# A gated linear attention with a GEGLU block: phase sums in the attention's PSUM banks, and another order of the table phases

## The chip, the core and the metric

The kernel runs on one core of one Trainium2 chip. The time is that of the device for one execution, in microseconds (us); before the change its median over three executions is 323.64 us (323.56 to 323.77).

The core has engines that each take their own instructions in order and wait for each other through semaphores: TensorE (PE; its weight loads are listed as PEld) multiplies matrices into PSUM, VectorE (DVE) does elementwise arithmetic, ScalarE (ACT) evaluates functions from a table that has to be loaded first, GpSimd (POOL) and SyncE (SP) mostly start transfers here.

## The reference

Attention first: a recurrence over 768 steps with a complex decay per channel, for 4 batches and 8 heads of 48 channels.

```python
mag = sqrt(a_re**2 + a_im**2)
scale = minimum(mag, 0.999) / (mag + 1e-6)
ar, ai = a_re * scale, a_im * scale
for t in range(S):                              # S = 768
    S_re, S_im = ar[t]*S_re - ai[t]*S_im + outer(k[t], v[t]), ar[t]*S_im + ai[t]*S_re
    y[t] = q[t] @ S_re
```

Then, on x = y laid out as 3072 tokens of 384 features (hidden size 1536):

```python
ffn = (gelu(x @ w_gate) * (x @ w_val)) @ w_out
out = x + sigmoid(x @ w_res) * ffn
```

## The kernel before

The recurrence is done in chunks of 128 steps. The decay of a chunk is a product of complex numbers, so its logarithm is a running sum: of ln|a| for the size, of the angle for the phase. Running sums along the 128 steps are matmuls with triangular matrices (`csl` for the logarithms, `cst` for the phases). The size becomes `E` and `Ei` (exponentials of plus and minus the sum), the phase is reduced to one turn (`r`, `fg`) and becomes cosine and sine (`CS`). Queries and keys are multiplied by both (`qE`, `kE`, then `Q`, `K`), and what is left is ordinary linear attention: transposes (`tp`, copied as `qk`), scores (`at`, masked as `atm`), the output `y`, the carried state (`dk`, `G`, `Gb`). After that `x` is transposed to `xT` for the gates.

A group g is two chunks of 128 steps, and there are 12 groups, 3 to a batch (`NS = 3`). They are handled in 7 units: one group, five pairs, one group. ScalarE needs three tables: ln/exp, trigonometric, gelu. The program alternates `phase_x(u)`, which has the ln/exp and the trigonometric table, and `phase_y(u)`, which has gelu. In `phase_x(u)` there stand the decay work of units u+1 and u+2, the second half of the attention of unit u and the output projection (`op`) of unit u-1; in `phase_y(u)` the gates `gp` and `vp` of unit u and the first half of the attention of unit u+1.

All eight PSUM banks are given out:

```python
psM = tile_pool(name="psM", bufs=4, space=PSUM)   # tag "mm": csl, cst, ms, tpx, gp, vp, rp, op
psT = tile_pool(name="psT", bufs=1, space=PSUM)   # tp
psA = tile_pool(name="psA", bufs=1, space=PSUM)   # at
psY = tile_pool(name="psY", bufs=1, space=PSUM)   # y
psD = tile_pool(name="psD", bufs=1, space=PSUM)   # dk
```

The steps for one group's decay; `s0` to `s3` belong to the ln/exp table:

```python
def s0(): act(out=lm, in_=lm, func=AF.Ln)                       # ar <- ar
def s1():
    act(out=s, in_=lm, func=AF.Exp, scale=-1.0)                 # s <- ar
    nc.vector.tensor_tensor(out=th, in0=s, in1=th, op=OP.mult)  # ai <- s,ai   (L189)
def s2(): act(out=s, in_=th, func=AF.Square)                    # s <- ai
def s3():
    act(out=s, in_=s, func=AF.Ln, bias=1.0)
    nc.vector.scalar_tensor_tensor(out=lm, in0=s, scalar=0.5, in1=lm, ...)    # L197
    nc.vector.tensor_scalar(out=lm, in0=lm, scalar1=LNMAX, ..., op0=OP.min)   # L198

def p1_arctan(g): act(out=th, in_=th, func=AF.Arctan)           # ai <- ai, trigonometric table

def cs_l(g, c):
    cs = psM.tile([128, DM], FP, tag="mm", ...)
    nc.tensor.matmul(out=cs, lhsT=lmat[c], rhs=lm[:, sl], start=True, stop=True)
    def ex():
        act(out=E[:, sl], in_=cs, func=AF.Exp)
        act(out=Ei[:, sl], in_=cs, func=AF.Exp, scale=-1.0)
    return ex

def cs_t(g, c):
    if c == 0:
        T["fg", g] = pE.tile([128, C * H, 2, D], FP, tag="fg", name="fg")
    cs = psM.tile([128, DM], FP, tag="mm", ..., name="cst")
    nc.tensor.matmul(out=cs, lhsT=tmat[c], rhs=th[:, sl], start=True, stop=(s == 0))   # L236
    if s > 0:                                                    # carry of the group before
        nc.tensor.matmul(out=cs, lhsT=ones2pi, rhs=T["P", g], start=False, stop=True)  # L238
    nc.vector.tensor_scalar(out=r, in0=cs, scalar1=MAGIC, scalar2=MAGIC, op0=OP.add, op1=OP.subtract)
    nc.vector.tensor_tensor(out=fg[:, hs, 1, :], in0=cs, in1=r, op=OP.subtract)
    if c == C - 1:
        ...   # absolute value of fg into fg[:, :, 0, :]   (L246)

def p2_sin(g):   # two activations Sin: CS[:, :, 0] and CS[:, :, 1] from fg
```

The attention of a chunk; each of these steps is issued with high priority, so that a scheduler moves it ahead of other work as soon as its inputs and buffers allow:

```python
def a():   # grp(hg), four heads
    tp = psT.tile([128, 1024], BF, tag="tp")
    ...    # 8 transposes of Q and K, copied to qk: one half by ScalarE, one by VectorE
    at = psA.tile([128, 4, 128], FP, tag="at", name="at")
    ...    # 4 matmuls
    nc.vector.tensor_tensor(out=atm, in0=at, in1=mask4, op=OP.mult)      # L359
...
def yy():
    y = psY.tile([128, DM], FP, tag="y", ..., name="y")
    ...    # 8 or 16 matmuls
    nc.scalar.copy(out=x, in_=y)
return [hi(f) for f in (enter, grp(0), dk, grp(1), yy)]
```

The gates of unit u need the `xT` of all its chunks:

```python
def gv_step(u, ffi):   # 12 times a unit
    ...    # 3 matmuls gp, 3 matmuls vp, both in "mm" banks
    act(out=h2[:, ffi, :], in_=gp, func=AF.Gelu)
    nc.vector.scalar_tensor_tensor(out=h2[:, ffi, :], in0=h2[:, ffi, :], scalar=0.5, in1=vp, ...)
```

The order in which steps are issued comes from `weave`, which spreads each list of steps over a stretch of the phase (0 to 1) and sorts all by place:

```python
atn = [table("trig_and_small")] + [call(p1_arctan, g) for g in g2]
cst = [call(carry, g) for g in g1] + [call(cs_t, g, c) for g in g1 for c in range(C)]
sin = [call(p2_sin, g) for g in g1]
...
weave((0.0, 0.12, csls), (0.05, 0.5, zip_steps([p1(g) for g in g2])), (0.01, 0.01, dec1), (0.12, 0.45, exs),
      (0.46, 0.46, dec), (0.2, 0.65, cst), (0.7, 0.95, atn + sin), (0.95, 0.95, dec3), (0.0, 0.8, att), (0.1, 1.0, ops))
```

From unit 3 on, the factor that carries the state (`M`) is made from three rows that go through DRAM and back (`decay0` to `decay3`, in the lists `dec1`, `dec` and `dec3`).

Of the kernel before, what the change touches and what calls it, by code (L numbers as in the profile page):

```python
# [9 lines left out]
FP = mybir.dt.float32  # L10
# [6 lines left out]
def weave(*streams):  # L17

    order = []
    for si, (begin, end, steps) in enumerate(streams):  # L20
        n = len(steps)
        for i, step in enumerate(steps):
            order.append((begin + (end - begin) * (i + 0.5) / n, si, i, step))
    for _, _, _, step in sorted(order, key=lambda e: e[:3]):
        step()
# [3 lines left out]
def kernel(  # L29
# [14 lines left out]
    B, H, S, D = q.shape  # L44
    DD = 2 * D
    DM = H * D
# [3 lines left out]
    C = 2  # L50
    W = C * DM
# [44 lines left out]
    pS = ctx.enter_context(tc.tile_pool(name="pS", bufs=2))  # L96
    pE = ctx.enter_context(tc.tile_pool(name="pE", bufs=2))
# [10 lines left out]
    psM = ctx.enter_context(tc.tile_pool(name="psM", bufs=4, space=PSUM))  # L108
    psT = ctx.enter_context(tc.tile_pool(name="psT", bufs=1, space=PSUM))
    psA = ctx.enter_context(tc.tile_pool(name="psA", bufs=1, space=PSUM))  # L110
    psY = ctx.enter_context(tc.tile_pool(name="psY", bufs=1, space=PSUM))
# [117 lines left out]
    def cs_t(g, c):  # L229
        s = g % NS  # L230
        th = T["th", g]
        if c == 0:
            T["fg", g] = pE.tile([128, C * H, 2, D], FP, tag="fg", name="fg")
        sl = slice(c * DM, (c + 1) * DM)
        cs = psM.tile([128, DM], FP, tag="mm", padded_shape=[128, 512], name="cst")
        nc.tensor.matmul(out=cs, lhsT=tmat[c], rhs=th[:, sl], start=True, stop=(s == 0))  # L236
        if s > 0:
            nc.tensor.matmul(out=cs, lhsT=ones2pi, rhs=T["P", g], start=False, stop=True)  # L238
        cs3 = cs.rearrange("p (h d) -> p h d", h=H)
        fg = T["fg", g]  # L240
        hs = slice(c * H, (c + 1) * H)
        r = pS.tile([128, H, D], FP, tag="r", name="r")
        nc.vector.tensor_scalar(out=r, in0=cs3, scalar1=MAGIC, scalar2=MAGIC, op0=OP.add, op1=OP.subtract)
        nc.vector.tensor_tensor(out=fg[:, hs, 1, :], in0=cs3, in1=r, op=OP.subtract)
        if c == C - 1:
            nc.vector.tensor_scalar(out=fg[:, :, 0, :].bitcast(mybir.dt.int32), in0=fg[:, :, 1, :].bitcast(mybir.dt.int32),  # L246
                                    scalar1=0x7FFFFFFF, scalar2=None, op0=OP.bitwise_and)
# [37 lines left out]

    def sums(g):
        ms = psM.tile([128, H], FP, tag="mm", padded_shape=[128, 512], name="ms")
        two = pS.tile([128, W], FP, tag="s", name="two")

        def half(gg, c):  # L290
            sl = T["lm", gg][:, c * DM:(c + 1) * DM].rearrange("p (h u d) -> p h u d", u=1, d=D)
            return sl.to_broadcast([128, H, 2, D])
        nc.vector.tensor_tensor(out=two.rearrange("p (h u d) -> p h u d", u=2, d=D), in0=half(g - 1, 1),
                                in1=half(g, 0), op=OP.add)
        for h in range(H):
            nc.tensor.matmul(out=ms[0:DD, h:h + 1], lhsT=two[:, h * DD:(h + 1) * DD], rhs=ones1,
                             start=(h == 0), stop=(h == H - 1), skip_group_check=True)
        T["ms", g] = mp.tile([128, H], FP, tag="ms", name="msb")
        nc.vector.tensor_copy(out=T["ms", g][0:DD], in_=ms[0:DD])
# [175 lines left out]
    def table(nm):  # L475
        def f():
            tab(nc.scalar.preload_act_table_set(nm))  # L477
        return f

    def gs(u):  # L480
        return UNITS[u] if 0 <= u < NU else []
# [7 lines left out]
    def call(f, *a):  # L489
        return lambda: f(*a)  # L490

    def zip_steps(lists):
        return [st[i] for i in range(max(map(len, lists), default=0)) for st in lists if i < len(st)]
# [14 lines left out]
    def phase_x(u):  # L508

        pend = []  # L510
        g1, g2 = gs(u + 1), gs(u + 2)
        d1 = [g for g in g1 if g % NS > 0 and g > NEAR]
        ops = [call(op_step, u - 1, jj) for jj in range(len(gs(u - 1)) * C)]
        att = att_steps(u, 1)
        if not g1:
            weave((0.0, 0.8, att), (0.1, 1.0, ops))
            return

        def csl(g, c):
            pend.append(cs_l(g, c))  # L520

        def ex():
            pend.pop(0)()

        def p1(g):
            return p1_steps(g) + ([call(decay0, g)] if g % NS > 0 and g > NEAR else [])
        csls = [call(csl, g, c) for g in g1 for c in range(C)]
        exs = [ex for _ in g1 for _ in range(C)]
        dec = [call(decay2, g) for g in d1]
# [3 lines that stand above are left out]
        dec1 = [call(decay1, g) for g in d1]  # L533
        dec3 = [call(decay3, g) for g in d1]
        table("natural_log_exp_and_others")()
        if u < 0:
            for f in [st for g in g1 for st in p1(g)] + csls + exs:
                f()
            for f in atn[:1] + [call(p1_arctan, g) for g in g1] + cst + sin:
                f()  # L540
            return
        dec3 += [call(sums_exp, g) for g in g1 if g % NS > 0 and g <= NEAR]
        if u == 0:
            sm = [[call(sums, g) for g in gg if g % NS > 0] for gg in (g1, g2)]
            weave((0.0, 0.25, zip_steps([p1(g) for g in g1])), (0.26, 0.3, csls), (0.31, 0.32, sm[0]), (0.35, 0.45, exs),
                  (0.4, 0.64, zip_steps([p1(g) for g in g2])), (0.641, 0.642, dec3), (0.645, 0.65, atn[:1]),
                  (0.65, 0.66, [call(p1_arctan, g) for g in g1]), (0.67, 0.85, cst), (0.75, 0.8, atn[1:]),
                  (0.9, 0.95, sin), (0.96, 0.97, sm[1]), (0.0, 0.5, att))
            return
        if u == 1:  # L550
            for f in dec3:
                f()
            dec3 = []
        weave((0.0, 0.12, csls), (0.05, 0.5, zip_steps([p1(g) for g in g2])), (0.01, 0.01, dec1), (0.12, 0.45, exs),
              (0.46, 0.46, dec), (0.2, 0.65, cst), (0.7, 0.95, atn + sin), (0.95, 0.95, dec3), (0.0, 0.8, att), (0.1, 1.0, ops))

    def phase_y(u):

# [34 lines left out]
    for u in range(-1, NU + 1):  # L593
        phase_x(u)
        while u >= 0 and T["a"] < min(NG, gs(u + 1)[-1] + 6 if gs(u + 1) else NG):
            load_a(T["a"])
        phase_y(u)
        for g in gs(u + 3):
            load_q(g)
            after_landing(T["k", g], call(load_v, g))  # L600
# [30 lines left out]
```

## Time and profile before

| stretch (us from the start) | what it is | length |
|---|---|---|
| 0 to 24 | first group's loads and decay | 24.0 |
| 24 to 63.2 | ln/exp and trigonometric tables of u = 0 | 39.2 |
| 63.2 to 83.5 | gelu table of u = 0 | 20.3 |
| 83.5 to 101.4, to 127.8 | table phase of u = 1, its gelu table | 17.9, 26.4 |
| 127.8 to 147.0, to 173.0 | the same for u = 2 | 19.2, 26.0 |
| 173.0 to 192.6, to 219.0 | u = 3 | 19.6, 26.4 |
| 219.0 to 236.3, to 262.6 | u = 4 | 17.3, 26.3 |
| 262.6 to 274.7, to 297.9 | u = 5 | 12.1, 23.2 |
| 297.9 to 322.4 | last projections and unit 6 | 24.5 |

The profiled execution spans 322.4 us. The stretches are those between the loads of ScalarE's tables (line L477), of which there are 21 of 1.283 us each.

A line of a group of instructions names line, engine, operation and tiles, then how many there are, their busy time and the mean of one in ns, and then the idle time of the engine just before them with what ended most of it. A line of the list of waits names who waited, for whom, the sum in us, how many times, and sometimes the longest. A releaser is inferred, and idle time of an engine that nobody waits for costs nothing.

### The profile page before, as it was taken

The numbers are of one execution on the slowest core, as the hardware profiler recorded it, in microseconds if no ns is written. First come the engines' busy times: TensorE is split into PE (matmuls) and PEld (weight loads), VectorE is DVE, ScalarE is ACT, GpSimd is POOL, SyncE is SP. The second block draws the span as 40 slices with busy tenths as digits, with TensorE's granted clock in tenths as the row PEclk, the third lists the DMA queues.
The fourth block names the chain that finished last, engine by engine and source line by source line (L and its number), as shares of the span: only waits on it lengthen the run. The fifth ranks groups of instructions, "written<-read, shape, count | busy, mean of one in ns | idle before, by whom it ended". The sixth has DMA issues, their size and how long they took to land.

```text
span 322.4 us, 5853 instructions
## 1 busy us (share of the span) xinstructions
PE 272.1 (84%) x2200; PEld 170.5 (53%) x2200; DVE 234.8 (73%) x431; ACT 209.8 (65%) x353; POOL 80.5 (25%) x115
## 2 busy tenths in 40 slices
PE   0337927789887999789997999998999999899994
PEld 0116624677543666445664556554656655555682
DVE  2446769968499995599982999974899837864352
ACT  4549684646998557977568976569665683656150
POOL 1206522022040370259020572000630003200220
PEclk9995676959999999999999999999999999999998
DMA  8999999989999995396850595000360003600441
GB/s 159 218 183 181 182 169 165 185 174 180 187 179 186 223 160 33 76 197 113 122 36 2 107 121 95 2 0 3 75 122 3 2 0 76 122 2 0 107 91 50
DMA packets 137755, 34.55 MB, mean 107 GB/s; under 512 B 126848, under 2 KB 137728, under 8 KB 137728
## 3 DMA queue, kind: packets, MB, share of 16 engines
q1 hardware_dynamic: 103296, 23.60, 36.8%
q0 software_dynamic: 34432, 10.59, 31.2%
q8 instruction: 17, 0.28, 0.3%
q14 instruction: 10, 0.08, 0.1%
HBM read 31.31 MB, written 9.07 MB: 125 GB/s over the span
## 4 chain that ended last, share of the span: by engine, by line
PE 56%; SPq 12%; ACT 11%; DMA 9%; DVE 6%; issue 3%; POOL 1%; ACTq 0%; DVEq 0%; POOLq 0%
PE vp L443 14%; PE gp L439 13%; SPq L136 6%; SPq L144 6%; PE op L463 6%; DMA k<-in_k_dram 4%; PE rp L455 3%; PE tp L349 3%; PE tp L346 3%; PE at L356 3%; ACT L477 3%; DMA m<-dm 3%; ACT s L124 3%; PE cst L236 2%; PE y L394 2%
## 5 line engine op out<-in xcount | busy, mean ns | idle before, releaser
L124 ACT ACTIVATE h<-gp 128x512 bf16<-128x512 f32 (+1 forms) x84 | 44.5, 536 | 38.4 <-PE gp L439 37.9
L439 PE MATMUL gp<-xT,wg 128*128 128x512 bf16 (+1 forms) x252 | 65.4, 353 | 3.4 <-ACT h L124 2.0
L443 PE MATMUL vp<-xT,wv 128*128 128x512 bf16 (+1 forms) x252 | 66.6, 353 | 0.0
L446 DVE SCALAR_TENSOR_TENSOR h<-h,vp 128x512 bf16<-128x512 bf16 (+1 forms) x84 | 49.8, 603 | 16.4 <-PE vp L443 12.0
L463 PE MATMUL op<-wo,h 128*128 128x384 bf16 x288 | 50.2, 326 | 8.1 <-ACT Ei L124 5.9
L463 PEld LDWEIGHTS <-h 128*128 128x128 bf16 x288 | 27.8, 98 | 28.7 <-issue 11.3
L351 ACT COPY qk<-tp 96x512 bf16<-96x512 bf16 x48 | 27.9, 580 | 17.1 <-PE tp L349 7.9
L359 DVE TENSOR_TENSOR atm<-at,mask 128x512 bf16<-128x512 f32 x48 | 32.9, 686 | 8.2 <-PE at L356 7.8
L472 POOL DMA_DIRECT2D out_dram<-x x22 | 20.4, 947 | 54.4 <-DMA out_dram<-ot 43.1
L439 PEld LDWEIGHTS <-wg 128*128 128x128 bf16 x252 | 23.7, 99 | 17.9 <-issue 4.2
L443 PEld LDWEIGHTS <-wv 128*128 128x128 bf16 x252 | 23.8, 99 | 13.3
L189 DVE TENSOR_TENSOR ai<-s,ai 128x768 f32<-128x768 f32 x12 | 11.1, 955 | 23.6 <-ACT s L124 23.6
L477 ACT ACT_TABLE_LOAD x21 | 26.9, 1283 | 1.1 <-PEq L615 0.7
L346 PE MATMUL tp<-ident,Q 128*96 128x128 bf16 x192 | 20.1, 231 | 6.9 <-DVE Q L321 6.2
L346 PEld LDWEIGHTS <-Q 128*96 128x96 bf16 x192 | 17.4, 130 | 15.3 <-DVE Q L321 10.0
L124 ACT ACTIVATE CS<-fg,hpi 128x768 bf16<-128x768 f32 x12 | 11.2, 935 | 20.8 <-DVE fg L246 20.7
L150 POOL DMA_DIRECT2D v<-in_v_dram x24 | 21.9, 932 | 4.2 <-DMA v<-in_v_dram 1.3
L349 PE MATMUL tp<-ident,K 128*96 128x128 bf16 x192 | 22.3, 235 | 0.0
L236 PE MATMUL cst<-ai,lt0b 128*128 128x384 f32 x24 | 11.8, 577 | 11.7 <-ACT ai L124 11.0
L352 DVE COPY qk<-tp 96x512 bf16<-96x512 bf16 x48 | 19.8, 413 | 2.3 <-ACT qk L351 1.7
L212 PE MATMUL csl<-ar,lt0a 128*128 128x384 f32 x24 | 11.4, 562 | 10.8 <-DMA ar<-in_a_re_dram 10.8
L466 DVE SCALAR_TENSOR_TENSOR ot<-sg,op 128x384 f32<-128x384 f32 x24 | 13.1, 547 | 10.1 <-PE op L463 10.1
(85 smaller groups left out, 522.0 us busy)
## 6 DMA issues: line engine op xcount, KB each, us to landing
ar<-in_a_re_dram SPq DMA_DIRECT2D x24, 192.0 KB, 4.7
ai<-in_a_im_dram SPq DMA_DIRECT2D x24, 192.0 KB, 4.1
q<-in_q_dram SPq DMA_DIRECT2D x24, 192.0 KB, 3.8
k<-in_k_dram SPq DMA_DIRECT2D x24, 192.0 KB, 3.7
out_dram<-ot SPq DMA_DIRECT2D x24, 192.0 KB, 2.5
out_dram<-x POOLq DMA_DIRECT2D x22, 192.0 KB, 3.7
v<-in_v_dram POOLq DMA_DIRECT2D x24, 96.0 KB, 5.0
wg<-in_moe_w_gate_dram POOLq DMA_DIRECT2D x4, 288.0 KB, 11.4
```

Of the source, the lines that this page charges most:

```text
L124: tab(nc.scalar.activation(**kw))
L150: nc.gpsimd.dma_start(out=t[:, c], in_=rows(v, g, c))
L346: nc.tensor.transpose(out=tp[0:DD, j * 128:j * 128 + 128], in_=Q(x), identity=ident)
L349: nc.tensor.transpose(out=tp[0:DD, 512 + j * 128:640 + j * 128], in_=K(x), identity=ident)
L351: nc.scalar.copy(out=qk[0:DD, 0:512], in_=tp[0:DD, 0:512])
L359: nc.vector.tensor_tensor(out=atm, in0=at, in1=mask4, op=OP.mult)
L439: nc.tensor.matmul(out=gp, lhsT=wg[:, fi, ffi * 128:(ffi + 1) * 128], rhs=xT[:, fi, :], start=(fi == 0), stop=(fi == KD - 1))
L443: nc.tensor.matmul(out=vp, lhsT=wv[:, fi, ffi * 128:(ffi + 1) * 128], rhs=xT[:, fi, :], start=(fi == 0), stop=(fi == KD - 1))
L446: nc.vector.scalar_tensor_tensor(out=h2[:, ffi, :], in0=h2[:, ffi, :], scalar=0.5, in1=vp, op0=OP.mult, op1=OP.mult)
L463: nc.tensor.matmul(out=ps, lhsT=h2[:, ffi, jj * 128:(jj + 1) * 128], rhs=wo[:, ffi, :], start=(ffi == 0), stop=(ffi == KF - 1))
L472: nc.gpsimd.dma_start(out=out[t0:t0 + 128, :], in_=T["x", token(u, jj)], accum_op=OP.add)
L477: tab(nc.scalar.preload_act_table_set(nm))
```

## The change

The phase sums leave the four shared banks. A group's first half goes to the bank of `at`, its second half to that of `y`, so that it need not wait for `csl` to be read. The temporary `two` of the sums of the first units takes a buffer of `fg` in place of one of `s`. And the table phases are woven differently: attention is listed first, exponentials lead the ln/exp table, the phase sums come early, the decay of the unit after next follows, and in the trigonometric table the sines stand ahead of the arctangents.

```diff
@@ cs_t
-        cs = psM.tile([128, DM], FP, tag="mm", padded_shape=[128, 512], name="cst")
+        if c == 0:
+            cs = psA.tile([128, 4, 128], FP, tag="at", name="cst").rearrange("p j t -> p (j t)")[:, 0:DM]
+        else:
+            cs = psY.tile([128, DM], FP, tag="y", padded_shape=[128, 512], name="cst")
@@ sums
-        two = pS.tile([128, W], FP, tag="s", name="two")
+        two = pE.tile([128, C * H, 2, D], FP, tag="fg", name="two").rearrange("p x u d -> p (x u d)")[:, 0:W]
@@ phase_x, u == 0
-            weave((0.0, 0.25, zip_steps([p1(g) for g in g1])), (0.26, 0.3, csls), (0.31, 0.32, sm[0]), (0.35, 0.45, exs),
-                  (0.4, 0.64, zip_steps([p1(g) for g in g2])), (0.641, 0.642, dec3), (0.645, 0.65, atn[:1]),
+            p12 = zip_steps([p1(g) for g in g2])
+            weave((0.0, 0.25, zip_steps([p1(g) for g in g1])), (0.26, 0.3, csls), (0.31, 0.32, sm[0]), (0.32, 0.5, p12[:-2]),
+                  (0.5, 0.58, exs), (0.6, 0.64, p12[-2:]), (0.641, 0.642, dec3), (0.645, 0.65, atn[:1]),
                   (0.65, 0.66, [call(p1_arctan, g) for g in g1]), (0.67, 0.85, cst), (0.75, 0.8, atn[1:]),
                   (0.9, 0.95, sin), (0.96, 0.97, sm[1]), (0.0, 0.5, att))
@@ phase_x, u > 0
-        weave((0.0, 0.12, csls), (0.05, 0.5, zip_steps([p1(g) for g in g2])), (0.01, 0.01, dec1), (0.12, 0.45, exs),
-              (0.46, 0.46, dec), (0.2, 0.65, cst), (0.7, 0.95, atn + sin), (0.95, 0.95, dec3), (0.0, 0.8, att), (0.1, 1.0, ops))
+        weave((0.0, 0.8, att), (0.0, 0.04, csls), (0.01, 0.01, dec1), (0.04, 0.2, exs), (0.05, 0.3, cst), (0.21, 0.21, dec),
+              (0.2, 0.6, zip_steps([p1(g) for g in g2])), (0.62, 0.95, atn[:1] + sin + atn[1:]), (0.65, 0.65, dec3),
+              (0.25, 1.0, ops))
```

## The prediction

> **What bounds the kernel now.** I read the page first: the busy times and the 40 slices.
>
> ```profile
> PE 272.1 (84%) x2200; PEld 170.5 (53%) x2200; DVE 234.8 (73%) x431; ACT 209.8 (65%) x353; POOL 80.5 (25%) x115
> ...
> PE   0337927789887999789997999998999999899994
> DVE  2446769968499995599982999974899837864352
> ACT  4549684646998557977568976569665683656150
> PEclk9995676959999999999999999999999999999998
> ```
>
> TensorE is the fullest engine, but 50 us of the span are not its own. About 18 of them lie in the first 24 us, before there is anything to multiply. What the change can touch is the rest. So I cut the span at the 21 table loads of ScalarE (line L477): each unit u has a ln/exp table, a trig table (together the "table phase") and a gelu table. The windows view of two such phases, each with the ln/exp part cut in two and the trig part third (columns: window, its length, busy us and count of PE, PEld, DVE, ACT, POOL, clock, DMA share, GB/s):
>
> ```profile
> 127.80:132.30 4.50, 2.77 (x12) 1.46 (x11) 0.00 (x0) 4.47 (x9) 0.46 (x1) 1.00 0.44 87
> 132.30:138.20 5.90, 5.79 (x29) 3.23 (x27) 5.88 (x8) 5.90 (x11) 2.00 (x4) 1.00 0.38 76
> 138.20:147.00 8.80, 7.38 (x42) 4.08 (x41) 8.36 (x20) 6.68 (x9) 5.77 (x10) 1.00 0.85 177
> 173.00:177.80 4.80, 3.02 (x13) 1.62 (x12) 0.21 (x1) 4.78 (x9) 0.52 (x1) 1.00 0.00 0
> 177.80:183.50 5.70, 5.59 (x28) 3.17 (x26) 5.70 (x9) 5.68 (x12) 3.37 (x5) 1.00 0.43 82
> 183.50:192.60 9.10, 8.40 (x48) 4.80 (x47) 8.37 (x21) 6.68 (x9) 6.77 (x10) 1.00 0.91 131
> ```
>
> VectorE does nothing for the first 4.5 us of the phase and is then full to its end. In the trig part ScalarE has room and waits. The list of waits (us in total, times, longest) says for whom:
>
> ```profile
> DVE ai L189 <- ACT s L124: 23.6, 5, 5.4
> ...
> ACT CS L124 <- DVE fg L246: 20.7, 10, 5.2
> ```
>
> The sine (CS) waits for VectorE to finish the reduction of the phase sum (r, fg), and VectorE stood idle because its first work of the phase was the product ai, which needs two ScalarE functions first. The gelu phase is different: from 147.0 to 173.0 TensorE is busy 25.9 of 26.0 us, and nothing but less work there shortens it. So a unit costs a table phase that is a chain through ScalarE and VectorE, plus a gelu phase that is TensorE alone.
>
> **What the Trainium skill says.** "ScalarE: Activation LUTs", section "What ACT_TABLE_LOAD costs", puts a load at about 1283 ns plus a drain of 1380 ns. The trace has 1283 ns, but the drain isn't seen: the load at 101.44 us is followed by an activation at 102.73. Both kernels have 21 loads, so this term doesn't move. "PSUM — Partial Sum Buffer", section "Engine vs sequencer instructions", says ScalarE and VectorE queues are strict FIFO and matmuls complete in program order. The trace agrees (one wait holds everything behind it), and my step for the first-gate delay rests on it. The same page's "Specifications (TRN2)" gives 8 banks of 2 KiB; the pools here take 4+1+1+1+1, all eight, so the phase sum can get no bank of its own and must borrow one. "TensorE: Matmul & The Clock Gate", section "What's actually happening", says an idle array runs at half clock: the phase sums at 50.24 us took 1.65 and 1.28 us a pair, and the later ones 0.65, after TensorE had stood idle 7.8 us.
>
> **The change part by part.** No arithmetic is added or removed. Durations, from the groups:
>
> ```profile
> L243 DVE TENSOR_SCALAR r<-cst 128x384 f32<-128x384 f32 x24 | 13.0, 550 | 3.5 <-PE cst L236 2.6 <-PE cst L238 0.7
> L244 DVE TENSOR_TENSOR fg<-cst,r 128x384 f32<-128x384 f32 x24 | 12.8, 548 | 0.1
> L359 DVE TENSOR_TENSOR atm<-at,mask 128x512 bf16<-128x512 f32 x48 | 32.9, 686 | 8.2 <-PE at L356 7.8
> L351 ACT COPY qk<-tp 96x512 bf16<-96x512 bf16 x48 | 27.9, 580 | 17.1 <-PE tp L349 7.9 <-PE y L396 5.1 <-PE dk L386 3.4
> ```
>
> Back to back they advance by some 0.08 us less than that (two ai of 0.955 take 1.83 together), so I count 0.47 for a 384-wide VectorE operation, 0.87 for a 768-wide one or a Q/K product, 0.60 for atm, 0.33 for a qk copy, 0.5 for the clamp (L198) and 0.3 for an xT copy.
>
> (1) *Early phase sums.* A unit with two groups has 4 r, 4 fg and 2 absolute values, 10 x 0.47 = 4.7 us. They no longer wait for the four "mm" banks that hold csl until the last exponential, and can run where VectorE was idle.
>
> (2) *Exponentials first.* All E and Ei come right after the ln/exp load, so qE and kE can start some 2.6 us into the phase (1.28 load, 0.1 to 0.2 small exponentials, three exponentials at 0.37) and not at 4.5.
>
> (3) *Sines before arctangents.* The sines need only fg, and arctangents (two, 1.5 us) feed the next unit alone. Q and K begin about 1.5 us earlier within the trig part.
>
> (4) *The price.* The borrowed banks belong to at (one buffer) and y (one buffer). The attention's second half is now ordered around the phase sums, and the built program's instruction order shows it: before, the whole attention stood in the gelu phases. Now part stands in the table phase, and in three units the next unit's first chunk too, ahead of the first gate matmul (gp). Small attention matmuls in each gelu phase, u = 0 to 4: before 170, 190, 182, 190, 190, after 138, 86, 146, 138, 102. One costs about 0.046 us: the gelu stage at 147.0 has 26.0 us, less 72 gp/vp at 0.216 (0.65 for three) and 12 rp at 0.163, leaving 8.5 us for 182.
>
> So gelu phases shrink by 1.5, 4.8, 1.7, 2.4 and 4.0 us. But gp needs the last xT copy, and VectorE must first get through what stands ahead of it. Counted along the built order, from the first qE to that copy: u=1: ten 768-wide (8.7), twelve 384-wide (5.6), two Gb (0.8), two clamps (1.0), four atm (2.4), four qk (1.3), xT: 20 us. u=2: 16.0, u=3: 15.5, u=4: 16.4 in the same way. With the start at 2.6 and 0.5 to 1 us of waits, first gp comes 23.6, 19.2, 19.0 and 19.5 us after the ln/exp load, against 15.8, 18.0, 18.3 and 16.0 before (99.30 less 83.52, and so on).
>
> The sum: u=1: +7.8 - 4.8 = +3.0. u=2: +1.2 - 1.7 = -0.5. u=3: +0.7 - 2.4 = -1.7. u=4: +3.5 - 4.0 = -0.5. The last table phase (262.65) gets 80 more small matmuls, and gp moves from about 13.3 to 16.5 us into it, while 28 x 0.046 = 1.3 leave what follows: about +1.8. In u=0 (24 to 63 us) the second pair of groups gets its ln chain before the exponentials, and ai stands ahead of qE and kE, which wait for late q and k. I count the trig load at 46.8 and not 48.05, and with sums drained through two banks behind cold matmuls the gelu load at 60.6 and not 63.24: -2.6; its gelu phase -1.5. Together -2.0.
>
> Last, the gelu phases are longer than their matmuls (27.8, 26.5, 27.0, 27.0 us from first gp to csl, against 26.3, 25.9, 26.3, 26.3 by count, 3.5 us in all), as attention waits stand among the gates. With roughly half of the attention gone I take half, -1.8 us, and a little for the M product, which waited 3.4 us for its transfer and gets it earlier. **-4.1 us: 319.5.**
>
> **The rivals.** *A: the sine wait is the bound, and its 20.7 us come back.* For: it is the largest ScalarE wait of the table phases and directly attacked. Against: TensorE's total stays; in the phases from 83.5 to 275 it has only some 12 us free (18 us less 14 busy at 83.5, 3.3, 2.6, 2.0). If most is filled, 308 to 313. *B: VectorE becomes the bound of the table phases.* It gets attention work (0.6 + 0.33 per four heads) just where it was full, and TensorE waits for xT: u=1 is the example. For: the counts above; against: the operations move rather than grow, and leave the gelu phase. If u=4 and the last phase behave as u=1, 326 to 330. *C: one-buffer banks make a new chain* at -> atm -> cst -> r, fg -> at on TensorE's in-order queue, with out-projection matmuls (op) between as filler. Some 1 us a unit: 324.
>
> **Range and chances.** My sum leans on long in-order queues with an error of about 1 us in each of six phases, and one large positive term. 312 to 327. Over 2% faster means under 317.2, which needs most of A: 0.31. Over 2% slower means above 330.1, all of B: 0.09. Within: 0.60.
>
> **What would show it right or wrong.** The sine's wait for fg should fall from 20.7 to under 8 us, VectorE should be busy in the first 4.5 us of each ln/exp table, and gelu stages should be shorter by 1.5 to 5 us while table phases are longer. u=1 (83.5 to 127.8, 44.3 us) should not gain; u=0 and u=3 should. It is wrong if TensorE's idle time in the table phases stays below 3 us with the attention in them (then A), or if gates wait over 3 us for xT in u=2 and u=3 too (then B).

## The result, and the profile after

The changed kernel takes 334.24 us (median of four runs, 332.08 to 335.06), the kernel before 323.63: a ratio of 1.0317 (95% interval 1.0268 to 1.0366). The prediction was 319.5, with 312 to 327 as its range. The profiled executions span 332.2 and 322.4 us.

The page of the changed kernel, busy times and slices:

```profile
PE 279.1 (84%) x2181; PEld 179.0 (54%) x2200; DVE 235.7 (71%) x431; ACT 208.5 (63%) x353; POOL 78.4 (24%) x115
...
PE   0336767699946999987999979999789999999995
...
DVE  2457727789598884699973999957989549754263
ACT  4559574537897345979557896568935476455250
...
PEclk9955655969985899999999999999979999999999
```

TensorE is busy 7 us longer with the same matmuls, and the row of its clock has 5 in more places: at half clock the 16 small matmuls `ms` of unit 0 took 2.72 us, at full clock, in the kernel before, 1.44. Before, all slices from 71.5 to 320 us had full clock; now the clock drops around 96 to 110 and 243 to 247 us as well.

The table phases of u = 2 and u = 3 again, cut at the same distances from the ln/exp load, and at the trig load (window, length, busy us and count of PE, PEld, DVE, ACT, POOL, clock, DMA share, GB/s):

```profile
134.20:138.70 4.50, 4.50 (x16) 2.55 (x15) 1.84 (x3) 4.49 (x11) 0.60 (x2) 1.00 0.46 91
138.70:148.94 10.24, 9.36 (x86) 5.78 (x85) 10.02 (x20) 7.79 (x13) 3.90 (x6) 1.00 0.85 155
148.94:155.33 6.39, 4.56 (x37) 2.64 (x36) 6.39 (x14) 6.36 (x9) 3.65 (x5) 1.00 1.15 126
179.76:184.56 4.80, 4.80 (x18) 2.72 (x17) 2.04 (x3) 4.79 (x12) 1.52 (x4) 1.00 0.01 1
184.56:192.28 7.72, 7.37 (x47) 4.09 (x45) 7.69 (x15) 6.37 (x10) 4.59 (x6) 1.00 0.65 110
192.28:199.42 7.14, 5.66 (x53) 3.69 (x55) 7.14 (x18) 7.11 (x11) 3.58 (x5) 1.00 0.93 135
```

VectorE does 1.8 to 2.0 us of work in the first stretch, where it did 0.0 to 0.2, and ScalarE no longer waits in the trig part (6.36 of 6.39 us). But the ln/exp part has grown from 10.4 to 14.7 us and from 10.5 to 12.5, and the trig part has shrunk only by 2.4 and 2.0. The list of waits says why:

```profile
ACT h L124 <- PE gp L442: 45.7, 64, 6.5
...
DVE qE L312 <- ACT E L124: 13.0, 4, 3.4
ACT CS L124 <- DVE fg L249: 12.9, 3, 7.5
```

The sine's wait is down from 20.7 us to 12.9; what is left lies in unit 0 and before it, and in units 1 to 5 it is gone. In its place VectorE waits for the first exponentials, and ScalarE for gates (37.9 us before).

What an operation costs has not moved (`r` and `fg`, too, take 551 and 550 ns), only where it stands. Two of the groups that the prediction priced, now with their waits:

```profile
L362 DVE TENSOR_TENSOR atm<-at,mask 128x512 bf16<-128x512 f32 x48 | 32.9, 686 | 7.4 <-PE at L359 7.0
L354 ACT COPY qk<-tp 96x512 bf16<-96x512 bf16 x48 | 27.8, 580 | 24.7 <-PE tp L352 13.8 <-PE y L399 6.2 <-PE dk L389 3.4
```

ScalarE's copy qk waits 24.7 us where it waited 17.1: the attention is the part that now stands badly.

Between two ln/exp loads lies one unit. Where the 9.8 us between the two profiles come from:

| unit | before | after | difference | predicted |
|---|---|---|---|---|
| 0 (start to the ln/exp load of u = 1) | 83.5 | 85.2 | +1.6 | -4.1 |
| 1 | 44.3 | 49.0 | +4.7 | +3.0 |
| 2 | 45.2 | 45.6 | +0.4 | -0.5 |
| 3 | 46.0 | 44.2 | -1.7 | -1.7 |
| 4 | 43.7 | 46.4 | +2.7 | -0.5 |
| 5 | 35.2 | 37.6 | +2.4 | +1.8 |
| rest | 24.5 | 24.2 | -0.4 | 0 |

The remaining -2.1 of the prediction was spread over the units. The first gate matmul came 15.8, 18.0, 18.3 and 16.0 us after the ln/exp load of units 1 to 4 before. Now it comes after 26.8, 19.5, 19.0 and 23.4; predicted were 23.6, 19.2, 19.0 and 19.5. Units 1 and 4 are those whose gates are late and whose clock drops. Unit 0 differs by up to 2.3 us between profiles of kernels with the changed order and banks in it (83.4 to 85.8): it took 85.2 to 85.8 us in the three where half clock cost TensorE 14.8 to 16.0 us of work, and 83.4 to 84.1 in three where it cost 11.7. The profile above is one of the long ones, so the change costs between 0 and 2 us in unit 0, and nothing finer is read from it.

### The profile page after: what moved, and what is told of

Read it like the earlier page. It is cut to its first block, busy times and chain, and to the rows that moved or that the text cites. A ratio compares the mean times of both kernels' runs of the same rounds, so it can differ in the third digit from the quotient of the medians.

```text
span 332.2 us, 5816 instructions
## 1 busy us (share of the span) xinstructions
PE 279.1 (84%) x2181; PEld 179.0 (54%) x2200; DVE 235.7 (71%) x431; ACT 208.5 (63%) x353; POOL 78.4 (24%) x115
## 4 chain that ended last, share of the span: by engine, by line
PE 55%; ACT 18%; issue 11%; DVE 11%; DMA 3%; SPq 2%; POOL 0%; DVEq 0%; ACTq 0%; POOLq 0%
PE gp L442 11%; PE vp L446 11%; PE op L466 7%; ACT L480 4%; ACT s L124 4%; PE tp L352 3%; PE rp L458 3%; PE tp L349 3%; ACT CS L124 3%; PE at L359 3%; PE csl L212 2%; PE ms L299 2%; PE dk L389 2%; PE cst L239 2%; DVE ai L189 2%
## 5 line engine op out<-in xcount | busy, mean ns | idle before, releaser
L442 PE MATMUL gp<-xT,wg 128*128 128x512 bf16 (+1 forms) x242 | 61.8, 351 | 1.0 <-ACT h L124 0.5
L446 PE MATMUL vp<-xT,wv 128*128 128x512 bf16 (+1 forms) x243 | 61.6, 351 | 0.3
L466 PE MATMUL op<-wo,h 128*128 128x384 bf16 x288 | 55.4, 332 | 0.0
L354 ACT COPY qk<-tp 96x512 bf16<-96x512 bf16 x48 | 27.8, 580 | 24.7 <-PE tp L352 13.8
L475 POOL DMA_DIRECT2D out_dram<-x x22 | 20.7, 958 | 68.5 <-DMA out_dram<-ot 64.8
L466 PEld LDWEIGHTS <-h 128*128 128x128 bf16 x288 | 27.5, 100 | 17.3 <-issue 2.6
L446 PEld LDWEIGHTS <-wv 128*128 128x128 bf16 x252 | 23.9, 99 | 15.9
L480 ACT ACT_TABLE_LOAD x21 | 26.9, 1283 | 1.1 <-PEq L620 0.7
L349 PE MATMUL tp<-ident,Q 128*96 128x128 bf16 x192 | 21.0, 238 | 5.4 <-DVE Q L324 4.5
L349 PEld LDWEIGHTS <-Q 128*96 128x96 bf16 x192 | 18.4, 137 | 12.5 <-DVE Q L324 6.4
L352 PE MATMUL tp<-ident,K 128*96 128x128 bf16 x192 | 23.4, 242 | 0.0
L312 DVE TENSOR_TENSOR qE<-q,E 128x768 bf16<-128x768 f32 x12 | 11.5, 954 | 16.6 <-ACT E L124 13.0
L150 POOL DMA_DIRECT2D v<-in_v_dram x24 | 21.5, 899 | 3.7 <-DMA wv<-in_moe_w_val_dram 1.3
L359 PE MATMUL at<-qk 96*128 96x128 bf16 x192 | 21.0, 235 | 1.5 <-DVE atm L362 1.1
L397 PE MATMUL y<-v,atm 128*128 128x48 bf16 x192 | 16.1, 188 | 7.2 <-DVE atm L362 4.4
L397 PEld LDWEIGHTS <-atm 128*128 128x128 bf16 x192 | 12.7, 98 | 15.5 <-DVE atm L362 10.2
```

The lines of the kernel that those rows point to most:

```text
L349: nc.tensor.transpose(out=tp[0:DD, j * 128:j * 128 + 128], in_=Q(x), identity=ident)
L352: nc.tensor.transpose(out=tp[0:DD, 512 + j * 128:640 + j * 128], in_=K(x), identity=ident)
L354: nc.scalar.copy(out=qk[0:DD, 0:512], in_=tp[0:DD, 0:512])
L359: nc.tensor.matmul(out=at[:, j], lhsT=qk[0:DD, 512 + j * 128:640 + j * 128], rhs=qk[0:DD, j * 128:j * 128 + 128], start=True, stop=True)
L397: nc.tensor.matmul(out=ys, lhsT=st["atm", hg][:, j], rhs=V(h), start=True, stop=first)
L442: nc.tensor.matmul(out=gp, lhsT=wg[:, fi, ffi * 128:(ffi + 1) * 128], rhs=xT[:, fi, :], start=(fi == 0), stop=(fi == KD - 1))
```

## The experiments

"Order" is the order in which the instructions stand on an engine. Where it is not said to be pinned, the scheduler made it anew for all engines, so such a run can differ in places that its edit does not name. All ratios are to the kernel before, on the same chip.

### The change in parts

**Phase sums back in the shared banks, both new orders kept.**

```diff
-        if c == 0: cs = psA.tile(...)   # bank of at
-        else:      cs = psY.tile(...)   # bank of y
+        cs = psM.tile(..., tag="mm", name="cst")
```

> The changed kernel with one part undone: the phase sums go back to the four shared banks; both weaves stay. Theory T (the borrowed banks tie the attention to the phase sums, so that attention stands in the table phases and the first gate of u=1, 4 and 5 comes 7 to 11 us later than it did; and in u=0 the sums ms wait for a shared bank that csl holds until the late exponentials): the attention is back in the gelu phases, u=1 to u=5 lose no more than 1 us together, u=0 keeps its loss of 2 to 3 us: 325 to 327 us. Rival W (the new order of the weaves costs the time whatever bank is used): 331 to 334 us.

Measured: 330.81 us, ratio 1.0229 (1.0161 to 1.0298). Far above theory T and 0.2 below W's range: without any borrowed bank the new orders cost 7 us. The first gate of unit 1 comes after 11.7 us here, earlier than before the change, and the unit still takes 48.2: a late first gate is not the only form of the loss.

**Borrowed banks alone, old orders.** The edit of `cs_t` alone, made in the kernel before.

> The kernel before with one part done: the phase sums borrow the banks of at and y; weaves as before. Theory T: some 30 small attention matmuls move into each table phase, TensorE waits there for fg and atm, and the first gates come later: 327 to 331 us. Rival W: 323 to 325 us.

Measured: 331.44 us, 1.0239 (1.0190 to 1.0288). As theory T says, 0.4 beyond its range: the banks alone cost 8 us. First gates come after 20.1, 22.5, 23.4 and 16.8 us. TensorE's timeline in unit 1 shows the price, a matmul of y that waits for the last reader of a phase sum in its bank:

```profile
97.38 0.22 PE L397 MATMUL y<-v,atm 128*128 128x48 bf16 x1 [3.81 <-DVE fg L247]
```

**Old order of unit 0, the rest changed.** The `weave` of `u == 0` as before.

> The changed kernel with the weave of u=0 as before (exponentials right after csl and ahead of the second pair's logarithms). Theory T: ms finds a bank early, no wait of 3 us for the last Ei and none for msb, the gelu load of u=0 comes 2 to 4 us earlier: 330.5 to 332.5 us. If the loss in u=0 came from the two-bank phase sums and a cold array instead: 333.5 to 334.5 us.

Measured: 332.65 us, 1.0269 (1.0230 to 1.0309). 1.6 us less than the changed kernel, at the edge of theory T; the two intervals overlap. Clearer is the profile: `ms` starts at 38.76 us without a wait (42.78 in the changed kernel), and the gelu load comes at 61.77, where the profiles with the changed order have 64.6 to 65.6.

**Old order of units 1 to 5, the rest changed.** The last `weave` of `phase_x` as before.

> The changed kernel with the weave of u=1 and later as before; banks borrowed and the new weave of u=0 kept. Theory T: u=0 loses 2.5 us, and the borrowed banks still cost in the units, though less, as the sums come late and not much attention is caught behind them: 328 to 332 us. Rival W: the units are as before and only u=0 loses: 326 us.

Measured: 333.39 us, 1.0299 (1.0247 to 1.0352). Above both theories: banks and unit 0 cost 9.8 us under the old order of units 1 to 5, and the new order there hardly adds to them.

**Phase sums in a bank of their own.**

```diff
-    psM = tile_pool(name="psM", bufs=4, space=PSUM)
+    psM = tile_pool(name="psM", bufs=3, space=PSUM)
+    psC = tile_pool(name="psC", bufs=1, space=PSUM)   # cst
```

> The changed kernel, with the phase sums in a bank of their own (taken from the four mm banks, of which three are left), so that they share nothing with the attention's at and y. Theory T (the borrowed one-buffer banks tie attention, phase sums and VectorE into one chain): the attention runs free of the phase sums again and the time falls to 326 to 331 us; the first gate matmuls of units 1 and 4, 26.8 and 23.4 us after the ln/exp load in the changed kernel, come 3 us or more earlier. Theory W (the new order itself costs it): 333 to 336, and with one mm bank fewer for the gates perhaps more.

Measured: 340.21 us, 1.0489 (1.0442 to 1.0535). Beyond both ranges, though W had allowed for more. In units 1 to 5 it takes 217.6 us, against 222.9 changed and 214.3 before, with the first gates of units 1 and 4 after 10.0 and 14.1; there theory T's sign is right. But unit 0 takes 97.3 us with three shared banks, 12 more. It cannot tell the theories apart.

**New order of units 1 to 5**, with the old banks and the old order of unit 0. The move of `two` is in this run as well.

> The kernel before, with the new order of the phases of units 1 to 5 alone: phase sums in the mm banks, and the old order in unit 0. The run with both new orders and the mm banks took 330.8 us. Theory 1 (the order of units 1 to 5 costs it: the ln/exp part grows since the product ai stands behind the phase sums on VectorE, and nothing fills the sine's wait): 328.5 to 330.5. Theory 2 (the order of unit 0, with its sums late, costs most): 324 to 326.

Measured: 332.56 us, 1.0261 (1.0203 to 1.0319). More than either range: this order, with `two` moved, costs 9 us.

**Exponentials and sines first, nothing else.** In the kernel before:

```diff
-        weave((0.0, 0.12, csls), ..., (0.12, 0.45, exs), ..., (0.7, 0.95, atn + sin), ...
+        weave((0.0, 0.04, csls), ..., (0.04, 0.2, exs), ..., (0.7, 0.95, atn[:1] + sin + atn[1:]), ...
```

> The kernel before with its own banks and its own place of the phase sums, and only two parts of the change: exponentials lead the ln/exp table, and sines come ahead of arctangents. If the part of the change that costs is the early phase sums (ai behind them on VectorE) and the banks, this is 321 to 324 us. If taking the arctangents out of the sine's wait is what costs, 325 to 328.

Measured: 328.48 us, 1.0124 (1.0100 to 1.0149). This part, the mildest, costs 4.9 us by itself, 0.5 beyond the second range. So 7.8 us (banks), 8.9 (order of units 1 to 5) and 4.9 (a part of that order) do not add to the 10.6 of the whole. That they overlap is shown; that each disturbs the same thing is not.

**The next unit's first attention without priority.**

```diff
-        return [hi(f) for f in (enter, grp(0), dk, grp(1), yy)]
+        return [hi(f) if pri else f for f in (...)]   # pri = second half, or u < 2
```

> The changed kernel, with the first-half attention of the next unit no longer given priority over the gates (from unit 2 on). Theory T2 (the next unit's first attention chunk, which stands ahead of the first gate matmul in the changed kernel, is what makes the gates late): first gate 2 us or more earlier in units 4 and 5, and 328 to 331 us. Rival: the gates are late for VectorE's copies anyway, and the time stays at 333 to 335.

Measured: 334.53 us, 1.0323 (1.0287 to 1.0359). The rival's number. First gates come 2.2 and 2.3 us earlier in units 1 and 4, and the time stays: the attention comes back among the gates, and from the first gate of unit 1 to the next csl it takes 23.7 us in place of 21.5.

### The clock of TensorE

In unit 1 of the changed kernel TensorE's timeline has three waits (start, duration of one, what; in brackets the idle time before it and its releaser):

```profile
95.66 0.20 PE L397 MATMUL y<-v,atm 128*128 128x48 bf16 x1 [2.03 <-DVE fg L247]
...
98.41 0.50 PE L427 MATMUL tpx<-ident,x 128*128 128x128 bf16 x3 [2.18 <-ACT x L402]
...
101.87 0.22 PE L397 MATMUL y<-v,atm 128*128 128x48 bf16 x1 [1.69 <-DVE atm L362]
```

From 96.3 to 110.0 us the clock is half. Busy time times the missing share of the clock is the work lost: 10.0 us in the kernel before, all in unit 0, and 22.0 in the changed one, 16.0 of it in unit 0 and 6.1 in units 1 and 4. Theory H: that is the difference.

For these runs the order of every engine was pinned to that of the kernel named, and matmuls of no use put into the waits. They multiply two constants into columns, or into a bank, that nobody reads; other engines wait for nothing new.

```diff
+        for _ in range(n):   # in TensorE's queue, at the place of a wait
+            nc.tensor.matmul(out=dk[:, 384:512], lhsT=ident, rhs=ident, start=True, stop=True)
```

**In units 1 and 4:**

> The changed kernel with the order of every engine pinned to that of the changed kernel, and 152 matmuls of no use (128x128 into unused columns of the dk bank) in the five places of units 1 and 4 where TensorE waits 1.3 to 2.2 us; before the half-clock stretches at 96.2 to 110.0 and 243.0 to 246.8 us. Theory H (the half clock that follows those waits is what makes units 1 and 4 late): the array keeps its full clock there, unit 1 (49.0 us between ln/exp loads) falls to 46 to 47 and unit 4 (46.4) to 45 or less, in all 330 to 332 us. Theory Q (the waits on ScalarE and VectorE alone make the units late, the clock only follows): 334 to 336.

Measured: 334.43 us, 1.0315 (1.0273 to 1.0356), as theory Q. But the units differ. H fails in unit 1: the long half-clock stretch is gone (3.4 us of it are left, 104.8 to 108.2), and the unit still takes 48.4, its first gate after 26.2. H holds in unit 4, which falls from 46.4 to 44.9, its first gate from 23.4 to 21.8. And units 2 and 3 grow by 1.4 and 1.1, each with a new half-clock stretch of 3.4 us (from 149.1 and from 193.5), which takes the gain back.

Such stretches come and go between the runs that keep the changed kernel's order in these units, and the time goes with them. Unit 2 takes 45.4 to 45.6 us in four profiles without one and 46.9 to 47.0 in three with one, unit 3 takes 43.7 to 44.3 and 45.4 to 45.5 in the same profiles, unit 4 takes 44.4 to 44.9 in four without and 46.4 to 46.5 in three with one. Where the work is the same as well, a stretch of 3.4 us costs 1.1 to 1.6 us.

**In unit 0 as well:**

> The same with 138 more in the four waits of unit 0 (0.8 to 3.1 us ahead of ms and of the phase sums). Theory H: the half clock from 41.5 to 59.0 and 65.5 to 72.5 us goes as well, the ms group takes 1.5 us in place of 2.72, and the kernel takes 326 to 329 us. Theory Q: as the run with units 1 and 4 alone, or longer.

Measured: 330.69 us, 1.0194 (1.0155 to 1.0234). 3.7 us less than without the 138; unit 0 takes 81.3 us, and 83.5 in the run above. H holds in unit 0, though 2 us short of its range. The first ms in the kernel before, at full clock:

```profile
39.21 1.44 PE L296 MATMUL ms<-ones,two 128*96 128x1 f32 x16
```

The changed kernel's first ms and phase sum:

```profile
42.78 2.72 PE L299 MATMUL ms<-ones,two 128*96 128x1 f32 x16 [3.13 <-ACT Ei L124]
...
51.12 1.65 PE L239 MATMUL cst<-ai,lt0b 128*128 128x384 f32 x2 [2.31 <-ACT ai L124]
```

and with the waits filled:

```profile
43.68 1.52 PE L299 MATMUL ms<-ones,two 128*96 128x1 f32 x16 [0.57 <-ACT Ei L124]
...
52.06 1.04 PE L239 MATMUL cst<-ai,lt0b 128*128 128x384 f32 x2
```

**The kernel before, warm in unit 0:**

> The kernel before, its order pinned, with 229 matmuls of no use in the waits of unit 0 (4.5 us ahead of the first attention, 7.8 us ahead of the phase sums, and three of 0.7 to 0.9 us ahead of the first gates). Theory H: the half clock at 23.5 to 37.2, 44.0 to 54.5 and 64.5 to 71.5 us goes, the phase sums take 0.65 us a pair in place of 1.5, and the gates of unit 0, which TensorE alone sets, lose 3 us: 317.5 to 321. Theory Q: 323 to 325.

Measured: 321.50 us, 0.9933 (0.9901 to 0.9964): 0.5 above theory H's range, and faster than both kernels. Its row of the clock, and the phase sum that took 1.65 us:

```profile
PEclk9996699999999999999999999999999999999998
```

```profile
50.24 0.91 PE L236 MATMUL cst<-ai,lt0b 128*128 128x384 f32 x2 [0.86 <-ACT ai L124]
```

Unit 0 takes 79.7 us in place of 83.5, and the whole 2.3 less. So the half clock of unit 0 costs both kernels, 3.7 us the changed one and 2.3 the old one. It is a cost, and the smaller part of the difference: 1.4 us of it in unit 0 and 0.6 and 1.6 in units 1 and 4 make 3.6 of the 10.6, an estimate from these runs. With the waits of unit 0 filled in both kernels, and in the changed one those of units 1 and 4 as well, that one is still 9.2 us slower (330.69 and 321.50), with the new half-clock stretches in units 2 and 3 again (from 148.0 and 192.4 us).

### Which queue makes the gates of units 1 and 4 late

**Less work on VectorE.** Left out, for the groups that units 1 to 4 prepare, is the end of the logarithm (`s3`); order pinned.

```diff
-            nc.vector.scalar_tensor_tensor(out=lm, in0=s, scalar=0.5, in1=lm, ...)
-            nc.vector.tensor_scalar(out=lm, in0=lm, scalar1=LNMAX, ..., op0=OP.min)
```

> The changed kernel, its order pinned, without the two VectorE operations that finish the logarithm of the magnitude (0.5 s + lm and the clamp, 0.87 and 0.5 us a group) for the groups that are prepared in units 1 to 4: 2.7 us less on VectorE in each of units 1, 2 and 3 and 1.4 in unit 4, all between the ln/exp load and the first gate matmul; nothing is taken from ScalarE or TensorE. It leaves out part of the computation. Theory B (with the attention in them, the table phases are set by VectorE, which must get through its queue before the last xT copy): the first gate comes 2 to 2.7 us earlier in units 1 to 3 and 1 in unit 4, and the kernel takes 325 to 328 us. Theory C (the chain at, atm, phase sums, y on one-buffer banks sets it, with VectorE one member of many): the first gates come less than 1 us earlier, 331 to 334 us.

Measured: 333.67 us, 1.0305 (1.0275 to 1.0334). First gates after 27.1, 19.5, 19.0 and 23.4: none is earlier. As theory C, and theory B fell. The windows from the trig load to the end of the gelu load in unit 1, changed kernel:

```profile
96.10:105.10 9.00, 4.58 (x53) 3.67 (x49) 8.44 (x13) 8.97 (x12) 0.00 (x0) 0.51 1.17 192
```

and with less work for VectorE:

```profile
94.64:103.63 8.99, 4.57 (x52) 3.66 (x48) 5.84 (x9) 8.96 (x12) 0.00 (x0) 0.55 1.38 198
```

VectorE is busy 2.6 us less, and the stretch is as long as it was: the work was replaced by waits, for the copies qk that ScalarE makes between sines. ScalarE is full in both.

**Less work on ScalarE.** Left out are the arctangents of the same groups.

> The changed kernel, its order pinned, without the arctangents of the groups that are prepared in units 1 to 4 (1.5 us of ScalarE in each of units 1 to 3 and 0.8 in unit 4, between the last sine and the gelu load); all else is as in the changed kernel. It leaves out part of the computation. With 2.7 us less on VectorE the gates came no earlier, so theory B fell. Theory D (from the trig load to the gelu load the attention's copies qk and x stand in ScalarE's queue between sines, arctangents and table loads, and ScalarE is busy 8.97 of 9.00 us there: its queue sets the gates): the first gate comes 1.2 to 1.6 us earlier in units 1 to 3 and 0.5 to 0.8 in unit 4; about 328.5 to 330.5 us. Theory C (the chain on one-buffer banks sets it whatever ScalarE does): first gates within 0.5 us of before, 333 to 334.5.

Measured: 331.23 us, 1.0226 (1.0193 to 1.0259), between the two theories. The trig parts of units 1 and 2 are 1.5 us shorter, those of 3 and 4 some 0.7. But no first gate of units 1 to 3 is earlier: they come after 27.2, 21.1 and 20.6, the last two 1.6 later, each with a new half-clock stretch (from 150.0 and 194.4 us). The runs with filled waits had such stretches there too, and with them first gates after the same 21.1 (21.2) and 20.6. The gate of unit 4 comes 2.1 earlier, after 21.3; the half clock at 243 us is gone there, and its going alone had given 1.6. Theory D is left with 0.5 us in unit 4, as much as it expected there, and with nothing in units 1 to 3.

**Both left out.**

> Both omissions at once, arctangents and the end of the logarithm. Theory D: as without the arctangents alone, 328.5 to 330.5, since VectorE has room. If the two engines take turns in setting it (each omission only uncovers the other): 2 to 4 us less than without the arctangents alone.

Measured: 330.51 us, 1.0193 (1.0155 to 1.0231). The upper end of theory D; VectorE's relief adds 0.7 us, which is within the noise. First gates after 26.9, 19.5, 19.0, 21.3, with no half clock in units 2 to 4.

**The copies of the table phases' attention on VectorE**, order left to the scheduler.

```diff
-                nc.scalar.copy(out=qk[0:DD, 0:512], in_=tp[0:DD, 0:512])
+                (nc.vector.tensor_copy if vec else nc.scalar.copy)(out=qk[0:DD, 0:512], ...)
-            nc.scalar.copy(out=x, in_=y)
+            (nc.vector.tensor_copy if vec else nc.scalar.copy)(out=x, in_=y)
```

> The changed kernel with the copies qk and x of the second-half attention (the half that stands in the table phases) made by VectorE in place of ScalarE, from unit 1 on; the order is the scheduler's own and differs from the changed kernel's in many places. Theory D: ScalarE's queue is shorter by some 2 us in each table phase and the gates come earlier: 326 to 331 us. If VectorE had been the bound after all: 335 or more.

Measured: 328.72 us, 1.0135 (1.0099 to 1.0171). In theory D's range: 5.5 us come back, the first gate of unit 1 after 20.7. But the order on TensorE is another too: there the gates of unit 1 stand ahead of unit 2's first attention.

**The copies alone, order pinned.** 24 copies change their queue, nothing else does.

> The changed kernel with the order of every engine pinned, and only the 24 copies qk and x of the second-half attention of units 1 to 4 taken out of ScalarE's queue and put into VectorE's, each where its input is ready; TensorE's order is that of the changed kernel. Theory D (ScalarE's queue with the attention's copies in it sets the first gates): first gate of unit 1 from 26.8 to 23 to 25 us, of unit 4 from 23.4 to 21 to 22, in all 328 to 331 us. If the 5.5 us of the run with the copies on VectorE came from its other order on TensorE (gates ahead of the next unit's first attention): 332.5 to 335.

Measured: 341.33 us, 1.0520 (1.0489 to 1.0551). Slower by 7 us and beyond either theory: theory D, as one queue, fell. Only one place for each copy in VectorE's queue was tried. The first gates come after 28.6, 20.5, 20.8 and 23.6.

**The same, warm in unit 0.**

> The same, with the 138 matmuls of no use in the waits of unit 0, which alone gave 3.5 us. If the half clock in unit 0 and ScalarE's queue in units 1 to 4 are separate causes, the two gains add: 3 to 4 us less than with the moved copies alone.

Measured: 335.06 us, 1.0346 (1.0322 to 1.0370), 6.3 less. The sign is right, the size beyond the range. Between the two profiles (337.2 and 333.1 us) 3.6 us lie in unit 0, as expected, and 0.6 elsewhere. The profiled execution of the moved copies was the fastest of its six (339.00, with 341.33 as the median), so these two profiles cannot show where the rest of the 6.3 lies.

**The other order, copies on ScalarE.** Order pinned to that of the 328.72 us run; its 30 copies go back to ScalarE.

> The order of every engine pinned to that of the run with the copies on VectorE (328.7 us), but with its 30 copies qk and x given back to ScalarE, each at the place in its queue where VectorE had reached it. It completes the square: changed order with ScalarE copies 334.2, changed order with VectorE copies 341.3, other order with VectorE copies 328.7. If TensorE's order (the gates of unit 1 ahead of the next unit's first attention) gave the 5.5 us: 327 to 331. If it takes both, the order and the free ScalarE queue: 332 to 336.

Measured: 337.99 us, 1.0425 (1.0383 to 1.0467). Beyond either expectation. The square:

| | copies on ScalarE | copies on VectorE |
|---|---|---|
| order of the changed kernel | 334.24 | 341.33 |
| order made for copies on VectorE | 337.99 | 328.72 |

Each order is good only with the queues that it was made for: moving the copies costs 7.1 us in the one, and moving them back 9.3 in the other. So neither ScalarE's queue nor the order, taken alone, explains the loss.

## Why the prediction was wrong, point by point

**The bound of the phases: read right.** In units 1 to 5 the sine's wait went, VectorE works early, and the gates got shorter where attention left them. From first gate to next csl, units 1 to 4 take 21.5, 25.3, 24.5 and 22.3 us; the count (26.3, 25.9, 26.3 and 26.3 less the matmuls moved, at 0.046) gives 21.5, 24.2, 23.9 and 22.3. The 3.5 us of waits among the gates fell to 1.8: the term of -1.8 was right. Units 2, 3 and 5 came within 0.9 us.

Three of its signs misled. The sine's wait is still 12.9 us in all, for unit 0 and before, and not under 8. From load to load the gelu stages of units 1 and 4 grew, from 26.4 and 26.3 us to 30.4 and 30.2, since their gates now come long after the load. And TensorE's idle time in the table phases of u = 2 and u = 3 is 2.7 and 1.8 us (length less busy in the windows above), under the 3 us that were to mean A; the phases nonetheless grew from 19.2 and 19.6 to 21.1 and 19.7, as what fills them was moved in.

Between -4.1 us predicted and +9.8 between the profiles lie 13.9. Unit 0 makes 5.7 of them, and the first gates 7.4 (those of units 1 and 4 alone 7.1).

**The first step that failed: unit 0.** "I count the trig load at 46.8 and not 48.05, and with sums drained through two banks behind cold matmuls the gelu load at 60.6 and not 63.24". They came at 48.93 and 65.57, and the -4.1 us of unit 0 became +1.6 (0 to 2 by the other profiles, whose loads came at 47.9 to 48.6 and 64.6 to 64.9). I had counted the ln chain and the phase sums and left out the sums ms, which still need a shared bank: csl holds all four until the exponentials, and these now come late. TensorE idles 3.13 us, its clock is half when it goes on, ms takes 2.72 us in place of 1.44, and M, kE and the carries stand behind it. With the old order of unit 0 the wait and 3 to 4 us of the late gelu load go; that the missing bank is all of this was only read from the trace. The cold matmuls that I took into account were nothing new: filling the waits of the old unit 0 gave 2.3 us too.

**The step that failed most: the first gate of units 4 and 1.** "With the start at 2.6 and 0.5 to 1 us of waits, first gp comes 23.6, 19.2, 19.0 and 19.5 us after the ln/exp load". VectorE's count was good in unit 4: from the first qE to the last xT copy 17.3 us, counted 16.4. VectorE's timeline has that copy here:

```profile
243.94 0.34 DVE L433 COPY xT<-tpx 128x384 bf16<-128x384 bf16 x1
```

and TensorE's timeline what stands between it and the gate:

```profile
242.86 1.54 PE L466 MATMUL op<-wo,h 128*128 128x384 bf16 x5
244.20 0.80 PE L389 MATMUL dk<-v,K 128*96 128x48 bf16 x8
244.83 0.49 PE L466 MATMUL op<-wo,h 128*128 128x384 bf16 x1
245.11 0.63 PE L349 MATMUL tp<-ident,Q 128*96 128x128 bf16 x4
245.54 0.63 PE L352 MATMUL tp<-ident,K 128*96 128x128 bf16 x4
245.97 0.63 PE L359 MATMUL at<-qk 96*128 96x128 bf16 x4
246.39 1.21 PE L466 MATMUL op<-wo,h 128*128 128x384 bf16 x6
247.44 0.38 PE L442 MATMUL gp<-xT,wg 128*128 128x512 bf16 x1
```

The copy is done at 244.28, the gate starts at 247.44: 3.2 us of the projection and of the next unit's attention, with half clock up to 246.5. With the waits of unit 4 filled, the copy ends as long after the load as here (20.3 us) and the gate follows after 1.55 us in place of 3.16:

```profile
244.09 0.34 DVE L443 COPY xT<-tpx 128x384 bf16<-128x384 bf16 x1
...
245.98 0.59 PE L452 MATMUL gp<-xT,wg 128*128 128x512 bf16 x2
```

So one half of these 3.2 us is work on TensorE that the prediction left out, and the other half went with the half clock. The prediction named that chunk, "ahead of the first gate matmul (gp)", and then set the gate to the end of the copy. Of the 3.9 us missed in unit 4 this is 3.2. In unit 1 the copy ended 25.3 us after the load, where 23.6 were predicted for the gate, and the gate came 1.5 later.

**The method behind it: one queue summed.** For unit 1 the sum over VectorE's queue came near the measured time, and was still not what sets it: with 2.7 us of that queue removed the gate came no earlier. A chunk of attention goes through TensorE, ScalarE and VectorE in turn, twice, and "PSUM — Partial Sum Buffer", section "Engine vs sequencer instructions", says the queues of ScalarE and VectorE are strict FIFO; the runs agree, since work taken out of one came back as waits for another. Rivals B and C were both seen as I had described them, B as a full VectorE in the trig part and C as the waits for fg and atm ahead of y, and each was put at one sum. I take them for parts of one chain; no run shows it, as no single term of it could be taken away on the chip.

**What stays open.** Shown is that the new orders and the borrowed banks each come with 7 to 9 us, that the two overlap, that the half clock costs 1.6 us in unit 4 and 0.6 in unit 1, that filling the waits leaves 9.2 of the 10.6 us, and that less work in VectorE's or ScalarE's queue does not bring the first gate of unit 1 forward. Why each part costs what it does is not shown. A rival stands: that an order made anew suits this kernel worse than the one it had, almost whatever is edited. The mildest edit lost 4.9 us, and the scheduler's order for another split of the copies gained 5.5; this speaks for the rival and does not decide. Which places in the three orders would have to change together was not found. The move of `two` was not tried by itself.

## What to carry to other kernels

In this kernel, work that goes through three in-order queues cost what its place in all three cost, and not what one of them had room for; a sum over the fullest queue says how long that queue is and not when its last result comes. When something is moved out of a stage that one engine fills (here 86 to 146 small matmuls were left of 182 to 190), ask for each of its buffers who reads it last, and count everything that stands between the last input and the next stage's first instruction on that instruction's own engine. Before reordering, look where TensorE stands idle for some us ahead of a chain of matmuls: filling such waits with useless ones gave the only run here that is faster than the kernel before. And look at what the clock then does in every later unit, since a gain in one was lost in two others.

## What the runs showed of the hardware

The half clock comes sooner than I had thought. "TensorE: Matmul & The Clock Gate", section "HAM oscillation — how this bites in real kernels", asks for no idle gaps over about 3.4 us. Here the clock dropped at 96.3 us, 0.7 us after a single wait of 2.03, and at 243.1, 1.0 us after one of 1.34 among many small matmuls; a wait of 1.78 us in the kernel before brought none. In the changed kernel the clock changes at 17.84, 38.32, 41.73, 58.80, 65.63, 72.45, 96.35, 110.00, 243.12 and 246.53 us, all whole multiples of 3.413 us apart. So where a wait falls on that grid may decide whether it brings a drop, which would explain that stretches come and go between runs; it was not tried. The busy time of the 3.4 us ahead doesn't tell when: 1.30 and 1.88 us before the two drops, but 1.62 us, of large matmuls, at 173.8 to 177.2 in the kernel before, without one. What is counted stays open.

Matmuls of no use do keep the clock: 229 of them in the waits of unit 0 leave one half-clock stretch of three there (27.0 to 37.2 us), and lost work falls from 10.0 to 3.7 us.
